# A recurrent attention with a feed-forward block: the place of one load in SyncE's queue, and the source of one small copy

## The chip, the core and the metric

The kernel runs on one core of a Trainium2 chip. The time is the device time of one execution in microseconds (us). An engine's name in the profile stands beside its role here: PE is TensorE (matrix products), PEld its weight loads, DVE is VectorE, ACT is ScalarE, POOL is GpSimd. SP is SyncE, which computes nothing here and issues most of the DMA transfers; its queue appears as SPq.

## The reference

```python
# q, k, v, alpha: (4, 8, 768, 48); alpha in 0.8 to 1.0
state = zeros((B, H, D, D))
for t in range(S):
    state = alpha[:, :, t, :, None] * state + einsum('bhd,bhe->bhde', k[:, :, t], v[:, :, t])
    y[:, :, t] = einsum('bhd,bhde->bhe', q[:, :, t], state)
x = y.transpose(0, 2, 1, 3).reshape(B * S, H * D)      # 3072 x 384
a = x @ w1                                             # 384 x 1024
b = x @ w2
out = ((a * b) @ w3) @ w_out                           # 1024 x 1024, 1024 x 384
```

All in float32; the four weights arrive as 64-bit floating-point numbers, which the kernel takes apart into float32 itself.

## The kernel before, in words

**Part one** goes through the sequence in N = 24 chunks of 128 tokens (six to each of the four batches, NCH = 6), all eight heads at once. For a chunk, `logs` takes the logarithm of alpha on ScalarE (L326), `decays` sums it along the tokens with a product on TensorE and takes exponentials e (L351, L352), and `decayed` multiplies k and q by them on VectorE (qk, L361). `transposed` turns qk on TensorE (L383) and ScalarE copies the result out (qkT, L385). `attention` makes the scores and the outputs (L466, L426) once the mask has been applied (ms, L473); ScalarE copies the outputs out (x, L446). `outer` adds to the state that is handed to the next chunk (L395, L405).

The main loop runs over steps n = 0 to 24, and each step works on several chunks at different stages. At its start it issues loads: v of chunk n + 2 (`load_v`, L160), alpha of chunk n + 5 (`load_a`, L148), k and q of chunk n + 4 (`load_kq`, L154, L155). `store` puts the outputs of an earlier chunk into a scratch in DRAM, xd (L307): from step 10 or so on four transfers per step. In steps 8, 11, 15 and 19 (`loads`) `load_x` reads a group of three chunks back as xT (L542). Near the middle of step n, `logs(n + 4)` reads the alpha that was issued one step before. Alpha's tile `ac` has two buffers, the tile `kq` three, v four, and x four.

In the same steps, pieces of the feed-forward block's gates are run in between (`run(pieces)`): products of split x with the split weights (L556). In `exact`, the first two parts of a product go to one PSUM bank and the third to another; ScalarE copies the first out (t, L565) and VectorE adds the second (L567), so a bank comes free when t is done. The finished piece ab goes to DRAM (L631), and raw weights are loaded in small portions (L238) and converted.

**The decays at the chunks' ends.** For every second chunk, 2, 4, 8, 10, 14, 16, 20 and 22, three rows are gathered in a small scratch in DRAM, `ends[n]`: the first row of e (L354), the last row of e of the chunk before (L356), and the first row of alpha itself (L322 for chunks 2 and 4, L333 for the other six). `load_ends` reads them back one value to a partition (dec, L369), GpSimd multiplies them (L412, L413), and `advance` applies them to the state (T, L414). GpSimd issues all these transfers, and it also makes a copy of v with the halves of the partitions exchanged (vt, L168) for `attention`.

**Order.** Each engine, and SyncE's and GpSimd's queues, work in the order in which the instructions stand, and each instruction waits for what it needs by semaphores. `after_marks` places an instruction on its engine behind another that has been marked; `mark["pool"]` is the last marked GpSimd instruction. A transfer on SyncE waits, beside its data and its buffer, for the transfer issued eight places before it, since the transfers take turns on eight semaphores.

**Part two** runs the remaining gates, folds w3 and w_out into one matrix and projects; it is a long row of products (L556).

Of the kernel before, what the change touches and what calls it, by code (L numbers as in the profile page):

```python
# [48 lines left out]
def kernel(  # L49
# [12 lines left out]
    nc = tc.nc  # L62
    B, H, S, D = q.shape
    C = 128
    DM = H * D
    DF = moe_w1.shape[1]
    NCH = S // C
# [13 lines left out]
    TURNED = 8  # L81
# [30 lines left out]
    def after_marks(*names):  # L112
        stack = ExitStack()
        for x in names:
            stack.enter_context(tc.issue_after(mark[x]))
        return stack
# [4 lines left out]
    ends = {n: dram.tile([3, DM], FP32, name=f"ends{n}") for n in range(2, N, 2) if n % NCH}  # L121
# [10 lines left out]
    def rows(src, n):  # L132
        b, c = divmod(n, NCH)
        return src[b, :, ds(c * C, C), :].rearrange("h p d -> p h d")

    def paired(n):
        return 2 <= n < PAIRED

    def load_a(n):
        if paired(n):  # L140
            if n % 2 == 0:
                b, c = divmod(n, NCH)
                x = pairs[n // 2 % 2]
                nc.sync.dma_start(out=x.rearrange("p h s d -> p h (s d)"), in_=alpha[b, :, ds(c * C, 2 * C), :].rearrange("h (p s) d -> p h (s d)", s=2))
                st["a", n] = st["a", n + 1] = x
        elif n < N:
            st["a", n] = inp.tile([C, H, D], FP32, tag="ac", name="ac", bufs=2)
            nc.sync.dma_start(out=st["a", n], in_=rows(alpha, n))  # L148

    def load_kq(n):  # L150
        if n >= N:
            return
        st["kq", n] = inp.tile([C, 2, H, D], FP32, tag="kq", name="kq")
        nc.sync.dma_start(out=st["kq", n][:, 0], in_=rows(k, n))  # L154
        nc.sync.dma_start(out=st["kq", n][:, 1], in_=rows(q, n))  # L155

    def load_v(n):
        if n < N:
            st["v", n] = vs[n % len(vs)]
            (nc.gpsimd if 2 < n < 8 else nc.sync).dma_start(out=st["v", n][:, :, 0:D], in_=rows(v, n))  # L160
# [121 lines left out]
    def fetch(ahead=3):  # L282
        while weights and len(begun) < ahead:
            begun.append(weights.popleft())
            next(begun[-1])
# [17 lines left out]
    def store():  # L303

        while later:
            dst, src = later.popleft()
            nc.sync.dma_start(out=dst, in_=src)  # L307
# [4 lines left out]
    def logs(n):  # L312
        if n >= N:
            return
        a = st.pop(("a", n))
        if paired(n):
            if n % 2 == 0:
                nc.scalar.activation(a, a, AF.Ln)
                st["la", n] = st["la", n + 1] = a
                b, c = divmod(n, NCH)  # L320
                if n in ends:
                    nc.gpsimd.dma_start(out=ends[n][2:3].rearrange("m (h d) -> m h d", h=H), in_=alpha[b:b + 1, :, c * C, :])  # L322
            return
        a = a.rearrange("p h d -> p (h d)")
        la = st["la", n] = work.tile([C, DM], FP32, tag="la", name="la")
        nc.scalar.activation(la, a, AF.Ln)  # L326
        if n >= LATE:

            t = st["la", n] = work.tile([C, 2, DM], FP32R, tag="la2", name="la2", bufs=1)
            nc.scalar.copy(t[:, 0], la)  # L330
            nc.vector.tensor_sub(t[:, 1], la, t[:, 0].bitcast(FP32))
        if n in ends:
            nc.gpsimd.dma_start(out=ends[n][2:3], in_=a[0:1])  # L333

    def decays(n):
        if n >= N:
# [172 lines left out]
    def attend_state(n):  # L509
        qkT = st.pop(("qkT", n))  # L510

        y = [bank()[:, 0:HP * C].rearrange("p (j c) -> p j c", c=C) for _ in range(2)]
        st["y", n] = y, [(half * HP + j, i, y[i][ds(DP * half, DP), j, :])
                         for j in range(HP) for i in range(2) for half in range(2)]
        if n % NCH:
            for j, i, to in st["y", n][1]:
                r = ds(DP * i, D)
                nc.tensor.matmul(to, Ts[n % 2][r, j, :], qkT[r, 1, j, :],  # L520
                                 start=(j % HP == 0), stop=False, skip_group_check=True)
# [18 lines left out]
    def load_x(g, queue=nc.sync):  # L540
        st["xT", g] = xp.tile([C, KM, TG], FP32, tag="xT", name="xT")
        queue.dma_start(out=st["xT", g], in_=xd[g].rearrange("(k p) t -> p k t", p=C))  # L542
# [82 lines left out]
    def gate(g, f):  # L625
        yield from (late_gate if late else early_gate)(g, f)
# [68 lines left out]
    def run(pieces):  # L695

        for _ in range(pieces):
            if not fill:
                return
            try:  # L700
                next(fill[0])
            except StopIteration:
                fill.popleft()
# [22 lines left out]
    FIRST = 6  # L726
# [3 lines left out]
    for n in range(N + 1):  # L730
        if n > TURNED:
            load_v(n + 2)
        if not 1 < n < FIRST:
            store()
        if n in loads:
            load_x(loads[n])
        if n != 1 and not 2 < n <= FIRST:
            load_a(n + 5)
        raws = (3, 3, 3, 3, 2, 2, 3, 3)[n] if n < 8 else 4
        for m in (n + 3,) * (n <= FIRST) + (n + 4,) * (n >= FIRST):  # L740
            load_kq(m)
            if 2 < n <= FIRST and m == n + 3:
                load_a(n + 5)
            if 1 < n < FIRST:
                store()
            if n < FIRST - 2:
                fetch(raws)
        if FIRST <= n <= TURNED:
            load_v(n + 2)
        if 0 < n <= TURNED:  # L750
            attend_state(n - 1)
        if n < TURNED:
            scores(n)
        else:
            attention(n)
        transposed(n + 1)
        if n == 1:
            decays(3)
            load_a(6)
            with after_marks(("e", 3)):  # L760
                logs(4)
        if n == FIRST + 1:
            run(2)
        if n < FIRST:
            with after_marks("pool"):
                load_v(n + 2)
        if n - 2 in begin and n > FIRST:
            g, tiles = begin[n - 2]
            with after_marks(("ms", n), ("qkT", n + 1)):
                split_x(g, 0)  # L770
            fill.extend(gate(g, f) for f in tiles)
        if n == FIRST:
            with after_marks("l", ("qkT", n + 1)):
                split_x(0, 0)
            fill.extend(gate(0, f) for f in begin[n - 3][1])
        pieces = ((3, 3, 2, 0) if n > FIRST + 3 else (0, 3, 3, 0))[(n - FIRST) % 4] if n >= FIRST else 0
        if n == 0:
            with after_marks(("qkT", 0)):
                logs(2)
            decays(2)  # L780
            with after_marks(("e", 2)):
                logs(3)
        early, ready = n < FIRST, len(thirds) if n > 2 else n // 2
        marks = (*[("qkT", n + 1)] * (n < N - 1), *[("qk", n + 1), ("ms", n)] * early, *["x3"] * (n - 2 in begin and n > FIRST))
        if n < N - 2 and n != FIRST:
            with after_marks(*marks):
                convert(2 if early else 1, raws)
        advance(n)
        turn_v(n)
        if n > TURNED:  # L790
            st.pop(("x", n - 1))()
        elif n:
            attend(n - 1)
        outer(n)
        if n > FIRST:
            third(ready)
        run(pieces > 0)
        if early:
            with after_marks(*marks):
                convert(1, raws)  # L800
        with after_marks(*[("ms", n)] * (n < 3)):
            decayed(n + 2)
        if not early:
            with after_marks(*[("qkT", n + 1)] * (n < N - 4)):
                logs(n + 4)
        if n == 4:
            load_x(0)
        convert(early and n > 0, raws)
        run(pieces > 1)
        if n:  # L810
            decays(n + 3)
        if n <= FIRST:
            third(ready)
        if 0 < n < FIRST:
            with after_marks(("e", n + 3)):
                logs(n + 4)
        if n == FIRST:
            with after_marks("x3", ("e", n + 3)):
                convert(2, raws)
        elif n < N - 2:  # L820
            convert(n == FIRST - 1 if early else n % 3 == 0, raws)
        if n == FIRST - 1:
            assert len(done) == 2 * KM
        run(pieces > 2)
        if n == N - 3:
            while begun:
                convert(1)
            weights.extend(load_out(j) for j in range(KF))
            fetch(4)
# [90 lines left out]
```

## Time and profile before

| | |
|---|---|
| time, three runs | 460.95, 461.75, 464.62 us (median 461.75) |
| profiled execution: time, span | 467.82 us, 466.1 us |
| mean granted TensorE clock | 0.996 of full speed |
| TensorE, weight loads | 448.6 us (96%), 425.3 us (91%) |
| VectorE, ScalarE, GpSimd | 362.8 us (78%), 277.4 us (60%), 96.0 us (21%) |
| DMA | 80.38 MB in 149,381 packets, 97,904 of them under 512 B |
| alpha loads in a tile `ac` | 18, 192 KB each |
| first alpha rows from tile `ac` | 6 of 1.5 KB, GpSimd |

Busy times are sums over the span, of overlapping engines. An entry such as "A <- B: 2.2, 1, 2.2" tells that A stood for 2.2 us in total, once, 2.2 us at the longest, until B ended. In a timeline the first two columns are the start and the length in us, and "x4" joins four like instructions. A row on SPq is the issuing of a transfer; how long the transfer then takes to land is listed with the DMA issues. The chain of waits follows the end of the program back, step by step, to what released each instruction.

### The profile page before, as it was taken

To read this page: it belongs to the slowest core of one execution; us is meant where nothing else is said; L and a number is where in the kernel's file an instruction comes from. 1 tells how busy PE (TensorE), PEld (TensorE's weight loads), DVE (VectorE), ACT (ScalarE), POOL (GpSimd) and SP (SyncE) were. 2 spreads that over 40 slices of the span, in tenths; PEclk is the share of its full clock that TensorE was granted. 3 is DMA by queue.
4 is the path that set the end of the run, shared out by engine and by line. 5 is a ranking of instruction groups with operands and counts; after the bars stand their busy time and mean duration, and the time that the engine had idled before them with its cause. 6 is when DMAs were issued, how large, how long until landed. Compare 5 with 4: busy or idle time off the path is not lost.

```text
span 466.1 us, 11166 instructions
## 1 busy us (share of the span) xinstructions
PE 448.6 (96%) x4296; PEld 425.3 (91%) x4296; DVE 362.8 (78%) x578; ACT 277.4 (60%) x544; POOL 96.0 (21%) x186
## 2 busy tenths in 40 slices
PE   4998899999899999999999999999999999999996
PEld 2676599889799999999999999999999999999996
DVE  2879896899578969899998899998641967766671
ACT  4685875867467654798875676765544543333330
POOL 6243242416311532022222111211110000000000
PEclk9999999999899999999999999999999999999999
DMA  9999999999897977587766447412114876655511
GB/s 173 257 214 219 233 216 198 238 209 208 169 209 160 202 165 206 170 235 201 233 192 191 133 124 193 145 46 93 51 35 144 244 219 184 186 167 161 171 51 52
DMA packets 149381, 80.38 MB, mean 172 GB/s; under 512 B 97904, under 2 KB 139120, under 8 KB 149328
## 3 DMA queue, kind: packets, MB, share of 16 engines
q1 hardware_dynamic: 143552, 64.44, 56.2%
q0 software_dynamic: 5776, 15.22, 11.1%
q8 instruction: 34, 0.56, 0.6%
q14 instruction: 19, 0.16, 0.1%
HBM read 57.58 MB, written 22.06 MB: 171 GB/s over the span
## 4 chain that ended last, share of the span: by engine, by line
PE 84%; DMA 6%; DVE 3%; ACT 3%; issue 1%; SPq 1%; DVEq 0%; ACTq 0%
PE bank L556 70%; PE bank L426 4%; DMA kq<-in_q_dram 3%; PE bank L383 2%; PE bank L466 2%; DMA ac<-in_alpha_dram 2%; PE bank L395 1%; DVE qk L361 1%; PE bank L342 1%; PE bank L345 1%; DMA kq<-in_k_dram 1%; PE bank L348 1%; PE bank L500 1%; PE bank L526 1%; DMA abd<-ab 1%
## 5 line engine op out<-in xcount | busy, mean ns | idle before, releaser
L556 PE MATMUL bank<-x,w 128*128 128x384 f32 x1152 | 209.7, 337 | 0.8 <-DVE ms L473 0.7
L556 PEld LDWEIGHTS bank<-x,w 128*128 128x128 f32 x1152 | 200.1, 188 | 2.8 <-DVE ms L473 1.3
L556 PE MATMUL bank<-w3o,ab 128*128 128x384 f32 x576 | 100.2, 336 | 0.0
L556 PEld LDWEIGHTS bank<-w3o,ab 128*128 128x128 f32 x576 | 99.9, 188 | 0.0
L581 ACT ACTIVATE bank<-bank 128x384 f32<-128x384 f32 x96 | 45.8, 477 | 38.0 <-PE bank L556 37.8
L565 ACT ACTIVATE t<-bank 128x384 f32<-128x384 f32 x64 | 31.4, 495 | 53.0 <-PE bank L556 53.0
L631 POOL DMA_DIRECT2D abd<-ab x45 | 25.8, 573 | 135.1 <-DVE ab L617 116.4
L682 DVE TENSOR_TENSOR ab<-abl,ab 128x1024 fp32r<-128x1024 f32 x24 | 29.4, 1223 | 12.0 <-ACT ab L681 11.9
L681 ACT ACTIVATE ab<-abl 128x1024 fp32r<-128x1024 f32 x24 | 25.5, 1060 | 20.4 <-PE bank L556 18.6
L556 PE MATMUL bank<-wo,w3T 128*128 128x384 f32 x192 | 35.9, 334 | 0.0
L617 DVE TENSOR_TENSOR ab<-bank,r 128x384 f32<-128x384 f32 x44 | 24.2, 550 | 14.0 <-ACT bank L581 6.4
L251 ACT ACTIVATE power<-power,rebias 128x512 uint32<-128x512 uint32 (+1 forms) x36 | 25.2, 701 | 16.6 <-DVE power L250 16.5
L556 PEld LDWEIGHTS bank<-wo,w3T 128*128 128x128 f32 x192 | 33.5, 188 | 0.0
L361 DVE TENSOR_TENSOR qk<-kq,e 128x768 f32<-128x768 f32 x24 | 23.2, 967 | 12.9 <-ACT e L352 8.1
L385 ACT COPY qkT<-bank 128x512 f32<-128x512 f32 x48 | 26.2, 599 | 9.5 <-PE bank L383 9.5
L567 DVE SCALAR_TENSOR_TENSOR o<-bank,t 128x384 f32<-128x384 f32 x24 | 13.4, 556 | 23.4 <-issue 14.1
L567 DVE SCALAR_TENSOR_TENSOR r<-bank,t 128x384 f32<-128x384 f32 x40 | 22.0, 552 | 10.6 <-ACT t L565 9.8
L683 DVE SCALAR_TENSOR_TENSOR ab<-ab,abl 128x1024 fp32r<-128x1024 f32 x24 | 29.2, 1217 | 0.0
L466 PE MATMUL bank<-qkT 48*64 48x128 f32 (+1 forms) x512 | 26.3, 254 | 2.2 <-ACT t L565 2.2
L254 DVE SCALAR_TENSOR_TENSOR power<-raw,power 128x512 uint32<-128x512 uint32 (+1 forms) x36 | 23.7, 657 | 4.0 <-ACT power L251 4.0
L466 PEld LDWEIGHTS bank<-qkT 48*64 48x64 f32 x512 | 23.8, 139 | 2.8 <-ACT t L565 2.5
L253 DVE SCALAR_TENSOR_TENSOR mant<-mant,rest 128x512 f32<-128x512 uint32 (+1 forms) x36 | 23.6, 655 | 2.5 <-ACT rest L246 2.5
(100 smaller groups left out, 702.0 us busy)
## 6 DMA issues: line engine op xcount, KB each, us to landing
abl<-abd SPq DMA_DIRECT2D x24, 512.0 KB, 4.8
abd<-ab POOLq DMA_DIRECT2D x45, 192.0 KB, 3.1
raw<-in_moe_w_dram SPq DMA_DIRECT2D x64, 128.0 KB, 3.4
raw<-in_moe_w_dram SPq DMA_DIRECT2D x12, 512.0 KB, 6.2
xT<-xd POOLq DMA_DIRECT2D x9, 576.0 KB, 4.8
kq<-in_k_dram SPq DMA_DIRECT2D x24, 192.0 KB, 5.2
kq<-in_q_dram SPq DMA_DIRECT2D x24, 192.0 KB, 5.3
out_dram<-o SPq DMA_DIRECT2D x24, 192.0 KB, 3.7
```

The lines of the kernel that those rows point to most:

```text
L251: nc.scalar.activation(power, power, AF.Relu, scale=2.0 ** 23, bias=rebias)
L361: mark["qk", n] = nc.vector.tensor_mul(qks[n % 3][:, :, :, 0:D], st.pop(("kq", n)), st.pop(("e", n)).rearrange("p i (h d) -> p i h d", h=H ...
L385: mark["qkT", n] = nc.scalar.copy(qkT[:, :, :, ds(DP * half, DP)], tp[half]).ins
L466: nc.tensor.matmul(sc[1][to, j, :] if late else sc[0][to, :, j, :], qkT[r, 0, j, ds(DP * late, DP)], q, start=True, stop=True)
L556: nc.tensor.matmul(p, w[part][i], x[part][i], start=start and part == parts[0] and i == 0, stop=stop and part == parts[-1] and i == n - 1, ...
L565: nc.scalar.activation(t, p1, AF.Copy, scale=(1.0 + 1.0 / P) * scale)
L567: nc.vector.scalar_tensor_tensor(to, p2, scale, t, op0=ALU.mult, op1=ALU.add)
L581: nc.scalar.activation(p, p, AF.Copy, scale=1.0 + 1.0 / P)
L631: (nc.gpsimd if late else nc.sync).dma_start(out=abd[g][:, f, :], in_=ab)
L681: nc.scalar.activation(t[:, 0], ab, AF.Copy, scale=1.0 - 2.0 ** -13)
L682: nc.vector.tensor_sub(t[:, 1], ab, t[:, 0].bitcast(FP32))
L683: nc.vector.scalar_tensor_tensor(t[:, 2], t[:, 0].bitcast(FP32), -1.0 - 1.0 / P, ab, op0=ALU.mult, op1=ALU.add)
```

## The change

From step 9, the tenth, on (n > TURNED = 8) `load_a(n + 5)` is called directly behind `load_v(n + 2)`, ahead of the stores and of the load of xT. For the earlier steps it stays where it was. And in `logs`, the first row of alpha for `ends[n]` is copied by GpSimd from the input in DRAM to the scratch in DRAM, instead of from the tile `ac`, and placed behind the last marked GpSimd instruction; for chunks 2 and 4 this source was in use already (L322).

```diff
         if n in ends:
-            nc.gpsimd.dma_start(out=ends[n][2:3], in_=a[0:1])
+            b, c = divmod(n, NCH)
+            with after_marks("pool"):
+                nc.gpsimd.dma_start(out=ends[n][2:3].rearrange("m (h d) -> m h d", h=H), in_=alpha[b:b + 1, :, c * C, :])
...
     for n in range(N + 1):
         if n > TURNED:
             load_v(n + 2)
+            load_a(n + 5)
         if not 1 < n < FIRST:
             store()
         if n in loads:
             load_x(loads[n])
-        if n != 1 and not 2 < n <= FIRST:
+        if n != 1 and not 2 < n <= FIRST and n <= TURNED:
             load_a(n + 5)
```

## The prediction

> **What bounds the kernel now.** I read the page first: TensorE is busy 96% of the span, and its row of slices is full except in the first half of the attention part. Two rows below it I read the granted clock and the share of the DMA engines.
>
> ```profile
> PE 448.6 (96%) x4296; PEld 425.3 (91%) x4296; DVE 362.8 (78%) x578; ACT 277.4 (60%) x544; POOL 96.0 (21%) x186
> ...
> PE   4998899999899999999999999999999999999996
> ...
> PEclk9999999999899999999999999999999999999999
> DMA  9999999999897977587766447412114876655511
> ```
>
> The reader is to see that TensorE sets the end, so that only a TensorE stop can give time back; that one slice (the eleventh, 116 to 128 us) has both a hole and a lower clock; and that the DMA engines are nearly full up to there. Next I listed what TensorE waited for from 85 to 192 us, the stretch that the change touches. Two entries are left, 0.7 us for a mask (L473, which no load ends) and this one:
>
> ```profile
> PE bank L466 <- ACT t L565: 2.2, 1, 2.2
> ```
>
> The stretches around it (start:end, length, then the busy time of each engine, the clock, the DMA share, GB/s) show what follows the stop:
>
> ```profile
> 110.00:119.73 9.73, 9.73 (x155) 8.74 (x151) 7.90 (x12) 5.39 (x12) 4.83 (x8) 1.00 0.87 199
> 119.73:121.96 2.23, 0.00 (x0) 0.00 (x0) 0.02 (x1) 0.95 (x3) 1.95 (x4) 0.93 0.91 179
> 121.96:125.00 3.04, 3.04 (x68) 2.75 (x70) 3.01 (x6) 1.88 (x5) 0.32 (x2) 0.50 0.83 154
> ```
>
> TensorE stands for 2.23 us, and then works 3 us at half clock. The chain of waits (start, length, what) names the cause: ScalarE works in order, its copy t (L565), which frees a PSUM bank, stands behind the logarithm of alpha (L326), and that waits for alpha of chunk 18.
>
> ```profile
> 114.99 1.17 SPq L307
> ...
> 116.75 4.24 DMA ac<-in_alpha_dram
> 121.05 0.38 issue
> 121.44 0.48 ACT t L565
> 121.96 0.48 PE bank L466 x2
> ```
>
> Last I read SyncE's queue at this place, and then the DMA issues (count, KB, us to landing) from 110 to 114 us:
>
> ```profile
> 111.23 1.02 SPq L238 DMA_DIRECT2D raw<-in_moe_w_dram  x1
> 112.35 0.38 SPq L631 DMA_DIRECT2D abd<-ab  x1
> 112.83 0.38 SPq L160 DMA_DIRECT2D v<-in_v_dram  x1
> 113.31 3.33 SPq L307 DMA_DIRECT2D xd<-x  x4
> 116.75 0.40 SPq L148 DMA_DIRECT2D ac<-in_alpha_dram  x1
> ```
>
> ```profile
> raw<-in_moe_w_dram SPq DMA_DIRECT2D x1, 512.0 KB, 6.8
> ...
> abd<-ab SPq DMA_DIRECT2D x1, 192.0 KB, 6.4
> v<-in_v_dram SPq DMA_DIRECT2D x1, 192.0 KB, 6.7
> ```
>
> This is step 13 (v of chunk 15, alpha of chunk 18). Alpha is issued last of these, 3.44 us after the first store (116.75 - 113.31); but what was issued ahead of it lands late as well: raw at 111.23 + 6.8 = 118.03, abd at 118.75, v at 112.83 + 6.7 = 119.53.
>
> **The change part by part.** In steps 9 to 18 (ten loads; later ones load nothing) alpha moves from behind the stores (and in steps 11 and 15 behind the load of xT) to directly behind v. No instruction is added on SyncE.
>
> *Alpha in step 13, the one that TensorE waits for.* Before, it lands at 116.75 + 4.24 = 120.99. After, it can be issued at v's next place, 113.31. The trace doesn't show how long it then takes, so I bound it. Best: the same 4.24 us, landing at 117.55, 3.44 us earlier than before; the logarithm (0.43) and t (0.48) are then done by 118.5, before TensorE runs dry at 119.73, and the stop is gone. Worst: not earlier at all, 0 us. Between them I take the nearest row, v, which stands directly ahead in the same queue: abd and v, of the same 192 KB, land 119.53 - 118.75 = 0.78 us apart, so alpha lands at 119.53 + 0.78 = 120.31, which is 0.68 us earlier. The stop shrinks from 2.23 to 1.55 us. It doesn't vanish, because the 512 KB of raw weights and abd are still ahead.
>
> *The half clock behind it.* The attention matmuls of this step run from 119.30 to 125.61, 6.31 us, where the same group two steps on takes 2.06 us (132.10 to 134.16). The excess is 4.25 us, of which 2.23 is the stop and 2.02 the slow clock. A stop of 1.96 us at 6.2 us (L383, waiting for qk) left the clock at 1.00, and so did one of 1.07 us at 34.7 us. 1.55 us lies on their side, so I take the 2.02 us as gained; the other bound is 0.
>
> For the clock a rule of the Trainium skill weighs in: "TensorE: Matmul & The Clock Gate", Part 1, puts the lowering of the clock behind an idle window of about 3.4 us that runs freely. Here the trace disagrees, since 2.23 us of standing was enough. By the page no shortening of this stop would touch the clock, and the sum would be the 0.68 us alone.
>
> Sum for alpha in the profiled execution: 0.68 + 2.02 = 2.70 us, with bounds 0 and 4.25.
>
> *The other nine alphas.* They land earlier too (step 11: v lands at 96.71 + 3.3 = 100.0, alpha at 99.80 + 5.3 = 105.1), and ScalarE's waits for them (1.94, 1.70, 0.76, 0.61 us) shorten. TensorE doesn't stand at any of these, so they are worth 0; they are the reserve that keeps a new stop away when TensorE comes 2.7 us sooner.
>
> *What the move pushes back.* The four stores of each step go out one row (about 0.4 us) later and land one alpha (about 0.8 us) later. Who waits for them: the x copies (L446), which have four buffers, so four steps of 7 us; and xT, which is issued at 99.32, takes about 4.4 and is first read at 110.59 (L548), cover of 6.9 us. Without cover it would be 0.8 us at three places. k and q of the same step keep their place behind all of these, so the row count ahead of them is the same. The alpha issue waits for the logarithm two chunks earlier, whose buffer it takes (105.39 for step 13), which is 7 us back, so it doesn't hold the queue.
>
> *Alpha's first rows DRAM to DRAM.* Six GpSimd issues (L333) change their source, for chunks 8, 10, 14, 16, 20 and 22. Landing is 4.0 us from the tile and 4.1 from DRAM (the two issues of L322 do this already); the issue itself 0.52 against 0.55 to 0.75, so at most 6 x 0.23 = 1.4 us of GpSimd, which is busy 21%. They no longer wait for the load: 17.2 us in five waits and probably the 7.7 us ahead of the fifth row below, all idle time of GpSimd. Behind one of them stood the copies vt, and behind these v on SyncE in step 16:
>
> ```profile
> 135.63 0.54 POOL L333 DMA_DIRECT2D ends<-ac  x1 [7.71 <-PE bank L395]
> 136.21 0.74 POOL L168 COPY vt<-v 64x192 f32<-64x192 f32 x2
> ```
>
> v's row there is 1.56 us long instead of 0.38; some 1.2 us of SyncE's queue come back. Nothing on TensorE waits there, so 0; it is more reserve. The new order behind the last GpSimd mark puts the row of chunk 8 behind that of e (46.64), so v of chunk 7 at 47.17 goes out about 0.6 us later; it lands near 53 and is used past 60. Also gone is SyncE's wait for the old row read before an alpha buffer is refilled; the longest-held case was the row issued at 105.37, landed at about 109.9, long before 113.3, so 0 gained.
>
> **Sum against the runs.** The profiled execution took 467.82 us (span 466.1 and 1.7 around it), so it would come to 465.1. The three runs without a profile took 460.95, 461.75 and 464.62: the profiled one is 6.07 above their median, and they spread by 3.67, near the 4.25 that the stop costs in all. I read this as runs with and without the stop, so the median carries about half of it: 2.70 / 2 = 1.35 us, 461.75 - 1.35 = 460.4 us. About 1%, 4.6 us, is what a measurement of this kernel can tell from no change.
>
> **The rivals.**
>
> *The stop isn't in the median run, or the queue hides the move.* Then the time is 461.7. For it: 6.07 us between the profiled and the median run, more than the whole stop; v itself lands only at 119.53, so the place in the queue may matter less than the 512 KB ahead. This is also the way in which the change doesn't do what it says: issued earlier, landed no earlier. Against it: alpha stands behind 192 KB of stores in every step, and one run lies at 464.62.
>
> The Trainium skill speaks for this rival in "DMA: Bandwidth & Descriptors", section "Issuing engines are not separate DMA queues": all issues end on the same 16 DMA engines and interleave. The DMA share of 0.87 to 0.91 around the stop agrees.
>
> *The stop goes entirely, and the median has it.* 461.75 - 4.25 = 457.5, and with the 0.7 us mask stop 456.8. For it: 3.44 us earlier issue against a stop of 2.23. Against: the late landing of v.
>
> *Slower: k and q fall behind.* v and alpha, both in 192-byte rows, now go out back to back, and the second of such a pair can be held on SyncE: alpha's issue took up to 2.65 us early in the kernel (34.16, behind k and q), against 0.39. If it costs 2.3 us in each step, SyncE, whose rows follow each other without a gap in steps 10 to 14, falls 5 x 2.3 = 11.5 us back. q of chunk 16 is issued at 110.60, lands at 114.2 and is used at 123.94 (L361): cover 9.7 us. From the fifth such step TensorE would stop at L383 for 1.8 us, and 2.3 more in each of two further steps, 6.4 in all: 461.75 + 6.4 - 1.35 = 466.8. Against it: alpha itself went out directly ahead of k and q before, so this pressure is only moved, and from 85 us on its median row is 0.40 us.
>
> *The clock falls all the same.* Then only the shorter stop is gained, 0.68 / 2 = 0.34: 461.4. For it: 1.55 us is nearer to 2.23 than a quiet place would be, and what sets the clock isn't shown. Against: the stop of 1.96 us at full clock.
>
> **How the numbers follow.** Forecast 0.36 (own range 459.0 to 461.2), clock all the same 0.09, hidden 0.25, whole stop 0.20, slower 0.10. Faster by over 1% (under 457.1) is most of the whole-stop case and a little of the forecast's tail: 0.22. Slower by over 1% is the last rival, 0.10; the rest, 0.68, is within 1%. The range goes from the whole stop with the mask (456.8) a little down for a median that moves by itself, 456.3, up past no change by half the spread of the three runs, 463.6, which leaves the slower case out.
>
> **What would show it.** Right: SyncE rows in the order v, ac, xd in steps 9 to 18; alpha of chunk 18 landing about 1 us behind v; the wait of L466 for L565 under 2 us or gone; no slice with a lower clock past the first; no GpSimd wait for ac. Wrong in size: alpha landing 4 us after its issue with no stop at all. Wrong altogether: longer SyncE rows of alpha and stops at L383 for qk, or the same stop at the same place.

## The result: slower by 1.2%, and the profile after

| | before | after |
|---|---|---|
| time, six runs each | 463.52 us (460.95 to 466.64) | 468.99 us (467.02 to 471.0) |
| ratio after / before | | 1.0124, interval 1.0095 to 1.0153 |
| profiled execution: time, span | 467.82 us, 466.1 us | 467.02 us, 465.3 us |

The change costs 5.5 us. The two profiled executions don't show it, because the one of before took longer than any of the six runs of before and the one of after is the fastest of its six. The page of after, the lines that answer to those shown of before:

```profile
span 465.3 us, 11144 instructions
...
PE 447.7 (96%) x4296; PEld 424.1 (91%) x4296; DVE 362.6 (78%) x578; ACT 277.4 (60%) x544; POOL 93.2 (20%) x186
...
PE   4997999999899999999999999999999999999996
...
PEclk9999999999999999999999999999999999999999
DMA  9999999989998987577765436412105975665511
```

The slice with the low clock is gone, and the DMA share has lost some of its nines. What TensorE waited for in this execution from 60 to 300 us (total, times, longest):

```profile
PE bank L558 <- DVE r L569: 1.1, 1, 1.1
PE bank L558 <- DVE ms L475: 1.0, 2, 0.8
PE bank L468 <- ACT t L567: 0.8, 1, 0.8
PE bank L468 <- DVE ms L475: 0.6, 1, 0.6
```

Lines up to L330 keep their numbers and those from `decays` on stand two or three lines further down than before (L466 is L468). The old stop has shrunk from 2.2 to 0.8 us, where 1.55 was forecast, but small ones have come up around it. SyncE's queue in step 13, the one that the prediction rested on (start, length):

```profile
112.41 0.38 SPq L633 DMA_DIRECT2D abd<-ab  x1
112.89 0.38 SPq L160 DMA_DIRECT2D v<-in_v_dram  x1
113.37 1.19 SPq L148 DMA_DIRECT2D ac<-in_alpha_dram  x1
114.61 4.09 SPq L307 DMA_DIRECT2D xd<-x  x4
118.74 0.44 SPq L154 DMA_DIRECT2D kq<-in_k_dram  x1
119.23 0.58 SPq L155 DMA_DIRECT2D kq<-in_q_dram  x1
```

Alpha stands directly behind v, as meant. The four stores behind it now take 4.09 us to issue, the first of them 2.66, and k and q go out behind that. The chain of waits of the same execution runs through just these rows (start, length, what):

```profile
114.16 0.40 SPq L148
...
114.61 2.66 SPq L307
...
118.74 0.44 SPq L154
...
119.23 4.05 DMA kq<-in_q_dram
...
123.41 0.09 DVE qk L363
...
124.28 0.56 DVE r L569
...
124.89 0.45 PE bank L558
```

A held store makes q late, VectorE waits for q, and TensorE for VectorE.

### The profile page after: what moved, and what is told of

The parts are those of the page before. It is cut to its first block, busy times and chain, and to the rows that moved or that the text cites. A ratio compares the mean times of both kernels' runs of the same rounds, so it can differ in the third digit from the quotient of the medians.

```text
span 465.3 us, 11144 instructions
## 1 busy us (share of the span) xinstructions
PE 447.7 (96%) x4296; PEld 424.1 (91%) x4296; DVE 362.6 (78%) x578; ACT 277.4 (60%) x544; POOL 93.2 (20%) x186
## 4 chain that ended last, share of the span: by engine, by line
PE 86%; DVE 5%; DMA 4%; ACT 2%; issue 1%; SPq 1%; DVEq 0%; ACTq 0%
PE bank L558 70%; PE bank L428 4%; DMA kq<-in_q_dram 3%; PE bank L385 2%; PE bank L468 2%; PE bank L397 1%; DVE qk L363 1%; PE bank L344 1%; PE bank L502 1%; DMA abd<-ab 1%; PE bank L350 1%; PE bank L347 1%; SPq L307 1%; DVE ms L505 1%; PE bank L528 1%
## 5 line engine op out<-in xcount | busy, mean ns | idle before, releaser
L558 PE MATMUL bank<-x,w 128*128 128x384 f32 x1152 | 209.7, 337 | 2.0 <-DVE r L569 1.1
L558 PEld LDWEIGHTS bank<-x,w 128*128 128x128 f32 x1152 | 200.2, 188 | 4.2 <-DVE ms L475 1.6
L558 PE MATMUL bank<-w3o,ab 128*128 128x384 f32 x576 | 100.2, 336 | 0.0
L558 PEld LDWEIGHTS bank<-w3o,ab 128*128 128x128 f32 x576 | 99.9, 188 | 0.0
L567 ACT ACTIVATE t<-bank 128x384 f32<-128x384 f32 x64 | 31.1, 491 | 55.2 <-PE bank L558 55.2
L558 PE MATMUL bank<-wo,w3T 128*128 128x384 f32 x192 | 35.8, 334 | 0.0
L558 PEld LDWEIGHTS bank<-wo,w3T 128*128 128x128 f32 x192 | 33.5, 188 | 0.0
L468 PE MATMUL bank<-qkT 48*64 48x128 f32 (+1 forms) x512 | 25.2, 247 | 1.5 <-ACT t L567 0.8
L468 PEld LDWEIGHTS bank<-qkT 48*64 48x64 f32 x512 | 22.7, 133 | 2.3 <-ACT t L567 1.0
```

Source lines behind the costliest of these rows:

```text
L468: nc.tensor.matmul(sc[1][to, j, :] if late else sc[0][to, :, j, :], qkT[r, 0, j, ds(DP * late, DP)], q, start=True, stop=True)
L558: nc.tensor.matmul(p, w[part][i], x[part][i], start=start and part == parts[0] and i == 0, stop=stop and part == parts[-1] and i == n - 1, ...
L567: nc.scalar.activation(t, p1, AF.Copy, scale=(1.0 + 1.0 / P) * scale)
```

## The experiments

Ratios are to the kernel before on the same chip, with the 95% interval; the diffs are against the changed kernel. "Rows in flight" is a count made from the trace's packet records: the rows of all transfers that SyncE had issued before the one in question, less those that had started. A row on SPq that is much longer than usual is called a hold. A load of v, alpha, k or q is 1,024 rows of 192 bytes; the stores of a step are 384 rows of 512 bytes.

### Which part it is, and two nearer profiles (e1 to e4)

e1 leaves the first rows on the tile; e2 leaves the order as it was; e3 and e4 are one more look at before and at after.

```diff
 e1, in logs
-            b, c = divmod(n, NCH)
-            with after_marks("pool"):
-                nc.gpsimd.dma_start(out=ends[n][2:3].rearrange(...), in_=alpha[b:b + 1, :, c * C, :])
+            nc.gpsimd.dma_start(out=ends[n][2:3], in_=a[0:1])
 e2, in the main loop
-            load_a(n + 5)
...
-        if n != 1 and not 2 < n <= FIRST and n <= TURNED:
+        if n != 1 and not 2 < n <= FIRST:
             load_a(n + 5)
```

> Only the order on SyncE is changed: alpha directly behind v from the tenth step on; alpha's first rows still go from the tile ac. Theory A (the order costs the time: stores and then k and q are held on SyncE behind v and alpha): ratio to before about 1.012, as for the whole change. Theory B (the copy from DRAM to DRAM costs it, by its place in GpSimd's queue or by its transfer): about 1.000, or below by up to 0.6%. Theory C (both halves needed): between 1.003 and 1.009.

> Only alpha's first rows are changed: DRAM to DRAM, behind the last GpSimd mark; SyncE's order is that of before. Theory A (SyncE's order costs the time): ratio 1.000 within 0.3%. Theory B (the copy costs it): about 1.012. Theory C: between 1.003 and 1.009.

> The kernel before once more, for a second profile: the first was of an execution of 467.8 us, above all timed runs. If the stop at alpha of chunk 18 is part of the usual execution, it is there again; if it was that execution's own, the time is 461 to 464 us and TensorE has no stop of 2 us past 60 us.

> The changed kernel once more, for a second profile: the first was of its fastest execution, 467.0 us. Expected 468 to 471 us. Theory A: TensorE's extra standing lies past 85 us, where SyncE's order differs. Theory B: it begins at 43 us, with the row of chunk 8.

Measured: e1 1.0077 (1.0043 to 1.0111), e2 1.0001 (0.9972 to 1.0029), e3 464.15 us with a span of 462.4, e4 470.54 us with a span of 468.8. The order alone slows the kernel, and the rows from DRAM to DRAM by themselves do nothing that can be measured. e1's middle value is only two thirds of the whole; the intervals of the two overlap, so whether the copy adds something on top of the order isn't told. e3 lies near the median of before and e4 1.5 us above that of after, so these two show typical executions better than the first pair.

What TensorE waited for from 60 to 300 us, first in e3 (before), then in e4 (after):

```profile
PE bank L426 <- issue: 1.2, 1, 1.2
```

```profile
PE bank L468 <- DVE ms L475: 3.7, 2, 3.1
PE bank L428 <- issue: 1.2, 1, 1.2
```

In e3 there is no stop behind a load at all, so the 2.2 us stop from which the prediction set out belongs to one execution. The stretch from 90 to 120 us (length, busy time of PE, PEld, DVE, ACT and POOL, granted clock, DMA share, GB/s), in e3 and in e4:

```profile
90.00:120.00 30.00, 30.00 (x517) 28.06 (x517) 27.57 (x53) 21.89 (x50) 10.81 (x20) 1.00 0.99 209
```

```profile
90.00:120.00 30.00, 26.92 (x481) 24.84 (x480) 24.65 (x46) 18.71 (x42) 9.31 (x16) 0.89 0.83 183
```

TensorE is full and the DMA engines are full in the first; in the second TensorE stands for 3.1 us, the mean clock is 0.89 and the DMA share is down to 0.83. SyncE's queue in step 10 shows where the two part. In e3:

```profile
87.11 1.75 SPq L160 DMA_DIRECT2D v<-in_v_dram  x1
88.97 1.95 SPq L307 DMA_DIRECT2D xd<-x  x4
91.02 0.39 SPq L148 DMA_DIRECT2D ac<-in_alpha_dram  x1
91.51 0.52 SPq L154 DMA_DIRECT2D kq<-in_k_dram  x1
```

and in e4:

```profile
88.19 0.37 SPq L160 DMA_DIRECT2D v<-in_v_dram  x1
88.65 0.53 SPq L148 DMA_DIRECT2D ac<-in_alpha_dram  x1
89.23 6.11 SPq L307 DMA_DIRECT2D xd<-x  x4
95.44 0.39 SPq L154 DMA_DIRECT2D kq<-in_k_dram  x1
```

The same four stores take 6.11 instead of 1.95 us of SyncE. By the count, 2,192 rows are in flight when the first of them starts in e4, and it is held for 3.45 us, until 289 of them are left. In steps 9, 11, 12 and 13 of e4 its row is 4.12, 1.44, 2.43 and 3.35 us long, each time with 2,160 to 2,350 rows ahead (a store that isn't held takes about 0.4). A store also waits for the transfer eight places before it, but that isn't the hold: it had landed at 86.12, 3.1 us before the store of step 10 began, and in the other four steps 2.0 to 5.3 us before. Before has holds as well, but those of 2 us and more fall on q, on k or on the store of ab, mostly at about 2,400 to 2,600 rows (k in step 9 of e3: 3.17 us at 2,565, let go when 99 of them were left). What is let go then differs: k itself adds 1,024 rows and q follows, while behind the held store come only small stores, so the engines run dry. Less than 0.3 of the DMA engines is busy for some 11.5 us of steps 9 to 17 in e4 and 6.2 us in e3 (in stretches of a quarter of a us; where they begin moves this by up to 1 us), and SyncE spends 33.4 and 19.7 us on the stores there.

The count isn't all of it. In fifteen of the traces, over these steps, 92 of the 139 rows that began with 2,150 or more in flight took over 1.2 us, but so did 110 of the 1,090 that began with fewer: v in step 10 of e3, shown above, 1.75 us at 1,174, and the fourth store of step 10 in e4, 1.66 us at 230. What holds those isn't shown.

### Which steps (e5, e6)

```diff
 e5 (e6: n < 13 in both places)
         if n > TURNED:
             load_v(n + 2)
-            load_a(n + 5)
+            if n >= 13:
+                load_a(n + 5)
...
-        if n != 1 and not 2 < n <= FIRST and n <= TURNED:
+        if n != 1 and not 2 < n <= FIRST and (n <= TURNED or not n >= 13):
```

> The whole change, but alpha goes ahead of the stores from step 13 on only; in steps 9 to 12 it stays behind them. Theory A1 (the loss is made in steps 9 to 12: the stores are held on SyncE behind two loads of 1,024 rows each, k, q and the store of ab come late, and VectorE waits for an ab buffer in step 12): ratio to before 0.997 to 1.003. Rival A2 (each step loses a little): about half the loss, 1.005 to 1.007.

> The whole change, but alpha goes ahead of the stores in steps 9 to 12 only. Theory A1: ratio 1.008 to 1.012, the whole loss. Rival A2: 1.004 to 1.006.

Measured: e5 1.0057 (1.0021 to 1.0093), e6 1.0083 (1.0056 to 1.0109). Either half is enough to slow the kernel, so no single transfer in a single step holds all of the loss. The two middle values add up to 1.4%, which the intervals can't tell from the whole. A queue that falls behind would do this: in e6 SyncE reaches v of step 13 at 117.2 us, where e3 does at 110.0, though from there on the order is that of before.

### Rows or bytes (e7, e8)

e7 is the changed kernel and e8 the order of before (with the rows from DRAM to DRAM), both with alpha of chunks 14 on read as 128 runs of 1,536 bytes. The bytes are the same and lie in the same part of the input, but the decays then belong to other tokens.

```diff
 in load_a, for n >= 14
-            nc.sync.dma_start(out=st["a", n], in_=rows(alpha, n))
+            flat = alpha[b].rearrange("h s d -> (h s d)")[ds(c * C * DM, C * DM)]
+            nc.sync.dma_start(out=st["a", n].rearrange("p h d -> p (h d)"), in_=flat.rearrange("(p x) -> p x", p=C))
```

> The whole change, and alpha of chunks 14 on is read as 128 runs of 1,536 bytes (the same bytes to the tile in another order, so the decays there are those of other tokens) instead of 1,024 rows of 192 bytes. Theory A1 (the many small rows of v and alpha in flight hold SyncE at the stores): the loss is gone, and the ratio to the next kernel is 0.996 to 1.003. Rival A3 (what counts is alpha's place itself: its wait for a buffer, the stores' place behind it, not its rows): the ratio to the next kernel stays near 1.010.

> The partner of the kernel above: the same 1,536-byte runs of alpha from chunk 14 on, alpha's first rows from DRAM to DRAM, and SyncE's order of before. Both theories: somewhat faster than before, ratio 0.985 to 0.998, since 10 x 896 rows of 149,381 packets fall away in a stretch where the DMA engines are nearly full.

Measured: e7 462.84 us, 0.9958 (0.9939 to 0.9978); e8 462.52 us, 0.9964 (0.9942 to 0.9987). With 128 instead of 1,024 rows the order is worth nothing either way. The penalty hangs on the number of rows of alpha (or the time that they take), not on its 192 KB.

### The place among the others (e9, e10)

e9 puts alpha at the head and v behind the stores, so that only one such load stands ahead of them; e10 puts v, alpha, k and q all ahead of the stores.

```diff
 e9
         if n > TURNED:
-            load_v(n + 2)
             load_a(n + 5)
...
-        if n != 1 and not 2 < n <= FIRST and n <= TURNED:
+        if n > TURNED:
+            load_v(n + 2)
+        elif n != 1 and not 2 < n <= FIRST:
             load_a(n + 5)
 e10
         if n > TURNED:
             load_v(n + 2)
             load_a(n + 5)
+            load_kq(n + 4)
...
-            load_kq(m)
+            if n <= TURNED:
+                load_kq(m)
```

> Alpha goes to the head of the step, as in the change, but v changes places with it: alpha, stores, v, k, q (and alpha's first rows from DRAM to DRAM). So alpha is as early as in the change, and only one load of 1,024 rows stands directly ahead of the stores, as before. Theory A1 (SyncE is held at the stores when the rows of two such loads are in flight ahead of them): ratio to before 0.995 to 1.003. Rival A3 (alpha's early place itself does the harm, by its wait or because the stores come after it): 1.008 to 1.013.

> The whole change, and from step 9 on k and q also go ahead of the stores: v, alpha, k, q, stores. Theory A1: SyncE is held at k or q, which put 1,024 rows in flight when it goes on, and then again at the stores; the DMA engines run dry less often than in the change, ratio 0.998 to 1.008. If what counts is that k and q come late behind held stores, it is at or below 1.000; if a hold anywhere costs the same, it stays at 1.012.

Measured: e9 0.9998 (0.9977 to 1.002), e10 1.0127 (1.0087 to 1.0168). Alpha ahead of the stores costs nothing if v isn't there too. In e10 the stores aren't what is held, but the load that comes third, k. Step 9 and the start of step 10 of e10 on SyncE:

```profile
78.83 0.69 SPq L160 DMA_DIRECT2D v<-in_v_dram  x1
79.62 0.86 SPq L148 DMA_DIRECT2D ac<-in_alpha_dram  x1
80.53 4.18 SPq L154 DMA_DIRECT2D kq<-in_k_dram  x1
```

4.18 us at 2,361 rows, and 3.02 in step 10 at 2,158. Whatever comes behind v and alpha can be held, whether it is long or short. That such loads stand back to back isn't enough by itself to cost time: alpha, k and q do so in before, and v, k and q in e9, with holds there too. The engines run dry, counted as above, for some 8 us in e10 and 4 to 5 us in e9; why the pair of v and alpha empties the queue further than the others isn't shown.

### Another queue (e11, e12)

```diff
 e11 (store takes its queue as an argument, SyncE by default)
-            store()
+            store(nc.gpsimd if 8 < n < 19 else nc.sync)
 e12, in load_a
-            nc.sync.dma_start(out=st["a", n], in_=rows(alpha, n))
+            (nc.gpsimd if n >= 14 else nc.sync).dma_start(out=st["a", n], in_=rows(alpha, n))
```

> The whole change, and from step 9 to 18 the stores are issued by GpSimd instead of SyncE, so SyncE's row is v, alpha, k, q, ab without them. Theory A1: ratio 0.995 to 1.003, unless GpSimd's own copies vt and T become late behind 2 us of issues per step (then TensorE waits for T or vt, up to 1.01). Rival A3: 1.008 to 1.013 with TensorE's stops where they were.

> The whole change, but from step 9 on GpSimd issues alpha at the same place of the program, so its rows are not in SyncE's ring. Theory A1: SyncE is not held at the stores, and the ratio is 0.995 to 1.003, or above if GpSimd issues alpha late because it waits for other work (then ScalarE waits for alpha at L326). Rival A3: 1.008 to 1.013.

Measured: e11 464.2 us, 0.999 (0.997 to 1.001); e12 462.9 us, 0.997 (0.9945 to 0.9995). Taking either side of the pair off SyncE takes the penalty away. e12 is better than both kernels, by 0.3% against before, and its interval only just leaves out 1. In the traces less than 0.3 of the DMA engines is busy for 2.2 us (e11) and 2.8 us (e12) of steps 9 to 17.

### By which link the late queue reaches TensorE (e13 to e18)

In e4 the chain of waits ran through the store of ab:

```profile
105.02 6.77 DMA abd<-ab
111.88 0.09 DVE ab L606
...
112.36 0.95 DVE qk L363
113.31 0.61 DVE ms L475
113.96 0.37 PE bank L468 x2
```

so my theory then was VectorE's wait for one of three ab buffers. e13 is the changed kernel with four, e14 the kernel before with four, e15 e12 with four; each with three x buffers in place of four.

```diff
-    abp = pool("abp", 3)
+    abp = pool("abp", 4)
...
-        x = work.tile([C, HP, 2, C], FP32, tag="x", name="x", bufs=4)
+        x = work.tile([C, HP, 2, C], FP32, tag="x", name="x", bufs=3)
```

> The changed kernel with four buffers for ab instead of three (and three for x instead of four, to make room). Theory A (the store of ab comes late behind the held SyncE, VectorE waits for its buffer in L606, and the mask ms and TensorE behind it): the waits of VectorE for abd go from 4.7 us in the changed kernel's typical execution to under 1 us, the holds of SyncE on the stores stay at 25 to 33 us in steps 9 to 17, and the time falls to within 0.6% of the kernel before (462 to 467 us where that takes 464). Theory B (the link is another one: the dry DMA engines bring x or the loads late, whoever waits for abd): the time stays at 1.010 to 1.014 of the kernel before, and with three x buffers TensorE's waits stand on x or xT.

> The kernel before with the same buffers (four for ab, three for x). Both theories: within 0.4% of the kernel before if the buffer of x that is given up costs nothing, since no VectorE wait for abd stands there. It is the base for e13: Theory A expects e13 over this run at 1.000 to 1.005, Theory B at 1.010 or more.

> The kernel with alpha of chunks 14 on issued by GpSimd (e12: 0.997 of the kernel before), with four ab buffers and three x buffers. Theory A: no wait for abd stands in e12, so the fourth buffer adds nothing and the time is that of e12, 0.995 to 0.999. Theory B: three x buffers cost as much as in e14, and this run stands as far above e12 as e14 above the kernel before.

Measured: e13 469.41 us, 1.0101 (1.0064 to 1.0139); e14 0.9999 (0.9974 to 1.0024); e15 0.9988 (0.9957 to 1.0018). e13's trace has no wait for abd left in these steps, and the time stays where it was. The theory that this buffer alone costs the time falls. e15 stands at 0.9988, so e12's small gain isn't seen a second time. Next I read, from the traces, when each product's mask ms starts on VectorE. Up to there all these traces keep within some 3 us of e3; the largest loss comes between the 31st mask (116.1 us in e3) and the 33rd (122.6):

| trace | v(15) issued | alpha(18) issued, landed | q(17) landed | 31st ms against e3 | 33rd ms against e3 |
|---|---|---|---|---|---|
| e3 (before) | 110.0 | 113.3, 117.3 | 119.2 | 0 | 0 |
| before, first profile | 112.8 | 116.7, 121.0 | 122.9 | -0.2 | +3.2 |
| after, first profile | 112.9 | 113.4, 119.1 | 123.3 | -0.9 | +2.7 |
| e4 (after) | 116.0 | 116.4, 122.7 | 126.5 | +2.3 | +5.9 |
| e1 | 115.9 | 116.4, 122.6 | 127.3 | +2.0 | +6.7 |
| e13 | 113.7 | 114.2, 119.0 | 123.7 | -2.0 | +3.1 |
| e10 | 113.6 | 116.6, 121.0 | 122.4 | -0.3 | +3.2 |
| e12 | 108.7 | 110.3, 116.4 | 118.6 | -1.2 | -1.2 |

The load that was moved forward lands later than in e3, because SyncE arrives at step 13 three to six microseconds late, and because it takes longer once it is issued (5.8 and 6.2 us against 4.0). ScalarE waits for it as the logarithm la, in e3, in after and in e4:

```profile
117.33 0.53 ACT L326 ACTIVATE la<-ac 128x384 f32<-128x384 f32 x1 [1.30 <-DMA ac<-in_alpha_dram]
```

```profile
119.15 0.52 ACT L326 ACTIVATE la<-ac 128x384 f32<-128x384 f32 x1 [4.03 <-DMA ac<-in_alpha_dram]
```

```profile
122.68 0.53 ACT L326 ACTIVATE la<-ac 128x384 f32<-128x384 f32 x1 [3.10 <-DMA ac<-in_alpha_dram]
```

The masks in the table are VectorE's. TensorE's own products, the same 4,296 in each trace, tell two links apart. Between the products that e3 starts at 110 and at 116 us, e4 goes from 1.1 us ahead of e3 to 4.8 us behind, at the stop that the store of ab makes and the half clock behind it, and loses nothing more up to 150; there the wait of 3.10 us for alpha costs TensorE nothing. e1 does the same (1.1 ahead, then 4.5 behind), and e6 nearly so (0.1 behind, then 3.8). After and e13, the fastest executions of their kernels, have no such stop and lose 2.7 and 3.9 us between 118 and 124, where TensorE waits for t and r, behind alpha and q. So the late queue reaches TensorE by different links in different executions.

The last three runs let GpSimd issue this one load: e16 is e13 with it, e17 the changed kernel with it, e18 the kernel before with it.

```diff
-            nc.sync.dma_start(out=st["a", n], in_=rows(alpha, n))
+            (nc.gpsimd if n == 18 else nc.sync).dma_start(out=st["a", n], in_=rows(alpha, n))
```

> The changed kernel with four ab buffers (e13) and with the one alpha of chunk 18, step 13, issued by GpSimd instead of SyncE. In e13 no wait for abd was left and the time stayed at 1.010; in its trace the mask of the 32nd product is 5.1 us later than in e3 from one step on, where ScalarE (L326) waits until alpha of chunk 18 lands at 119.0. Theory C (two links of the same weight: the ab buffer in step 12 and this alpha in step 13; the alpha itself lands later because SyncE's queue runs late): with both taken away the time is 0.998 to 1.004 of the kernel before, and alpha of chunk 18 lands 2 to 3 us earlier. Theory D (SyncE is late as a whole, and the next load or store behind it takes the place of any link that is removed): 1.007 to 1.012.

> The changed kernel with only the alpha of chunk 18 issued by GpSimd, three ab buffers as there. Theory C: the link of step 13 (3.6 us in the changed kernel's two profiles) is gone, that of the ab buffer is left in the executions that have it: 1.002 to 1.007 of the kernel before. Theory D: 1.009 to 1.013. If it is the alpha alone: 0.998 to 1.002.

> The kernel before with only the alpha of chunk 18 issued by GpSimd. It is the base for e17: Theory C and D both expect 0.995 to 1.001, since the typical execution of before (e3) has no stop of TensorE there, and its profiled one (467.82) a stop of 2.23 us that would be gone; a median of 0.997 would say that such stops are in the median of before.

Measured: e16 1.0037 (1.0014 to 1.006), e17 1.0031 (1.0006 to 1.0057), e18 0.9997 (0.9975 to 1.0019). By the middle values, taking one of the ten loads off SyncE removes about three quarters of the loss: 1.24% goes down to 0.31%, while the kernel before gains nothing from the same edit. The intervals allow anything from some two fifths to nearly all of it. A fourth ab buffer on top of that (e16) brings nothing more. The holds are still there in e17: SyncE spends 28.0 us on the stores in steps 9 to 17. In e17's trace alpha of chunk 18 lands at 112.5, q of chunk 17 at 121.5, and the 33rd mask is 1.0 us behind e3. What VectorE still waits for there, from 85 to 155 us:

```profile
DVE ab L606 <- DMA abd<-ab: 3.4, 2, 2.1
DVE r L569 <- ACT t L567: 3.3, 3, 1.4
DVE qk L363 <- DMA kq<-in_q_dram: 2.0, 2, 1.5
```

What stays open: e17 does two things, it brings this alpha in early and it takes 1,024 rows from in front of the stores, k and q of step 13 (the stores take 1.95 instead of 4.09 us). How the 0.9% divides between ScalarE's wait for alpha and VectorE's wait for q isn't told apart; the chain of after names q, the wait of 4.03 us alpha. Counted at TensorE's products, e17 loses 1.5 us at the first of the two places above and 0.7 at the second. e16, where alpha lands early too, at 114.7, loses 3.6 us at the first and 0.3 at the second. Why the first place costs e4 5.9 us and weighs so little in e17's median isn't shown, nor which wait makes up the last 0.3%.

## Why the prediction was wrong, point by point

**Where it set out.** "I read this as runs with and without the stop, so the median carries about half of it" was wrong. e3 has no such stop, and e18, which brings that alpha in at 115.5 by another queue and leaves the order of the rest, leaves the median where it was (0.9997, interval 0.9975 to 1.0019, where a gain of 1.35 us would be 0.9971). So the 1.35 us of gain were not there to be had; that was the first rival's first half. In the 21 runs of before that stand beside e1, its time ranges from 461.5 to 467.0 us.

**Alpha in step 13.** The relation was right: alpha lands 0.6 us behind v in after (119.1 and 118.5), where 0.78 was forecast, and the wait of L468 for L567 is 0.8 us. The anchor was wrong: I let alpha go out "at v's next place, 113.31", with v landing at 119.53 as in that one execution. Against e3, where alpha lands at 117.3, the move made it 1.8 us later in after and 5.4 in e4.

**The clock.** Stops of 1.1 us and less leave it at 1.00 in after, as forecast. In e4 the stop of 3.08 us is followed by half clock (length, busy times, clock, share, GB/s):

```profile
110.88:113.96 3.08, 0.00 (x1) 0.00 (x0) 2.08 (x4) 1.05 (x3) 0.53 (x2) 0.81 0.80 151
113.96:119.00 5.04, 5.04 (x96) 4.80 (x97) 5.04 (x8) 2.83 (x8) 2.13 (x3) 0.50 0.91 232
```

The 0.81 in the first row says that the clock had already fallen inside the stop, and the 0.50 behind it makes the stop dearer by some 2.5 us (half of 5.04, an estimate). The Trainium skill ("TensorE: Matmul & The Clock Gate", Part 1) puts the lowering behind an idle window of about 3.4 us; this trace disagrees again, with 3.08 us. In e6 a stop of 1.94 us at 112.0 is followed by 3.41 us of half clock from 115.45 on, so a stop of 1.55 us wasn't as safe as the prediction had it. Its comparison with "a stop of 1.96 us at 6.2 us" that left the clock at 1.00 doesn't hold either. The trace's clock record begins only at 15.8 us, and the page counts the time before it as full speed. But sixteen products of L383 take 1.11 us at 8.16, as the same ones do at half clock in e4 (1.12 at 117.36), against 0.72 at 18.46. So the clock was low there already.

**What the move pushes back: the step that failed.** It was costed at 0: "The four stores of each step go out one row (about 0.4 us) later", and "k and q of the same step keep their place behind all of these, so the row count ahead of them is the same". The count over a whole step is the same, but what counts for SyncE is the number of rows in flight at one moment. v, the stores and alpha in turn give the DMA engines some 2 us between two loads of 1,024 rows; v and alpha together put about 2,050 rows into the queue within 1 us. The stores then took up to 6.11 us where 1.95 had been, and everything behind them, abd, q and the next step's v and alpha, came late by what had been held. Its size, in place of 0, is the whole result, 468.99 - 463.52 = 5.5 us (467.78 - 464.31 = 3.5 us for the order alone, e1).

**The other nine alphas.** Not worth 0: e6 changes only steps 9 to 12 and costs 0.8%. The queue carries the lateness from one step to the next until it meets a transfer that has no slack: the store of ab in step 12 in e4, the loads of step 13 in after.

**DRAM to DRAM.** Costed at 0, measured at 1.0001 by itself (e2).

**The rival on the other side** had the right pressure, two loads of 192-byte rows back to back, and 466.8 us, which is 1.1% over the 461.75 from which I started. Its row at 34.16 even shows the condition: 2,199 rows were in flight there. It had only 0.10 because of the argument that "this pressure is only moved", which is the same error as above. It had the lateness of q right, but was wrong on what is held (it took alpha's own row, and it is the row behind) and on where TensorE feels it: not at the transposes (L383, now L385), but in the products of the gates and the scores (L558, L468), behind VectorE's waits for q and for the ab buffer and ScalarE's for alpha.

**The rule cited for the first rival.** "DMA: Bandwidth & Descriptors" of the Trainium skill, section "Issuing engines are not separate DMA queues", adds that issuing from several engines saves only the sequencer's time, usually small beside the transfer. Here that time was not small: SyncE spent 33.4 us of some 73 on the stores in steps 9 to 17 of e4, and e11 and e12, which only use a second queue, stand at 0.999 and 0.997.

## What to carry to other kernels

In this kernel, moving a load ahead in a full queue didn't bring it in earlier once it stood directly behind another load of many small rows, ahead of small stores. So count the rows that are in flight at that moment, not the rows of the step, and look at what stands behind. A queue whose rows follow each other without a gap has no free place in it; what took the penalty away here was taking a load off it (e12) or making its rows longer (e7). And a stop that one profiled execution shows isn't in the median until a second execution or a run that takes it away has shown it there.

## What the runs showed of the hardware that I had not expected

With 2,150 or more rows in flight, SyncE was held for over 1.2 us in about two of three issues (92 of 139), and with fewer in one of ten (110 of 1,090). The longest hold is 4.4 us (the first store of step 9 in e6). It is the next transfer that is held, even one of 144 rows, and its own size isn't what decides when it goes out: in e4 the first store of step 9, of 192 rows, was let go when 100 of the 2,348 rows ahead of it were left, and in e3 k, of 1,024, when 99 of 2,565 were. So a short store can wait as long as a long load, and adds far fewer rows when it goes; the DMA engines then have little to do until the next load is out. Other holds end earlier (the store of step 11 in e4 with 1,022 rows left). What decides how far the queue empties isn't shown.
